# Attention into a mixture of experts on one core: the bank of halved weights built three groups apart with GpSimd's subtractions, the lists filled in the prologue, the list tiles' weights loaded before their rows

## The chip, the cores and the metric

One Trainium2 chip, one of its cores. The metric is the device time of one execution in microseconds (us); the median of three runs is compared. The core has five engines with a queue of instructions each: PE (matmuls), DVE (VectorE), ACT (ScalarE), POOL (GpSimd) and SP, which here issues DMAs only. Each works through its queue in order, and an instruction that waits holds up all that stand behind it on its engine.

## The reference

Attention over pooled keys, then a mixture of 8 experts in which each token goes to one expert.

```python
# 4 batches of 12288 tokens, width 128; kv pooled 4x4 to 768 keys per batch
kv_flat = kv_pool.reshape(B, -1, C) @ w_sr;  k = v = kv_flat
s = scale * (q @ k.transpose(0, 2, 1))
a = np.exp(s - s.max(-1, keepdims=True));  a /= a.sum(-1, keepdims=True) + 1e-09
x = (a @ v).reshape(49152, 128)
logits = x @ w_gate;  e_idx = np.argmax(logits, axis=1)          # 8 experts
probs = softmax(logits);  eom = sigmoid(x @ w_output_gate)
for e in range(E):                                               # F = 1024
    h = np.maximum(x[mask] @ w1[e], 0.0);  ye = h @ w2[e]
    out[mask] = gate_w[mask, None] * eom[mask, e, None] * ye
```

## The kernel before

The tokens are taken in 96 **groups** of 512; four groups make a **chunk** of 2048, six chunks a batch. The outer loop goes over groups `i`, each in 8 slots `s`. In group `i` the kernel computes the scores and exponentials of group `i` (`qk`, four tiles of 128 tokens), the values of group `i-1` (`pv`), the router's logits of group `i-2`, and the experts' two matmuls of group `i-8` (`moe_h`, `moe_y`), so that attention and experts of different groups share the engines. Every fp32 operand is carried as two fp16 **halves**, the rounded value and the rest; a product is three matmuls. In a tile of scores, ACT takes the exponential (`pr`, L384) and the rounded half (`ph`, L390), POOL the rest (L391), and SP transposes both through a DMA (`PT`, L401). In the experts, ACT makes `HH` (L710) and DVE `HL` (L711) from each block of PE's results; the PSUM pool `psH`, with three buffers, holds these blocks and those of `pv`, and PE can't start a block before DVE has read the one that held its buffer.

Each chunk is computed densely with the one expert that most of its tokens chose; the tokens that chose another are written as rows into **lists** in DRAM (`scr`) by 16 indirect DMAs of POOL per chunk (`scr<-rw,idx`, L588, at most one a slot, only in slots in which the counter `spare` is zero), and after the last chunk the lists are worked off in **list tiles** of 128 rows. `fill` first writes a neutral row everywhere in the lists; before the change it is a generator that begins in group 8 and issues one of its eight DMAs every third slot, and routing does not issue the first row's DMA before all eight are out (`FILLED`).

The routing of chunk `c` (small DVE operations) runs in groups `4c+5` and `4c+6` and yields the expert `ei`. `w_load` then fetches that expert's weights. For the first `NDW` chunks it fetches the raw fp32 weights and `w_split` halves them in group `4c+7`: DVE takes the largest magnitudes (L629 on `wr`), PE turns them, DVE makes a power of two (L153 to L159), ACT scales (L662) and rounds (L670), POOL subtracts (L672). Later chunks fetch ready halves from the **bank** in DRAM: `w_bank` makes the halves of all eight experts once, while the first chunks run. Its steps for one expert: two DMAs, four reductions on DVE (L629 on `wb`), the power of two, then four times ACT's rounding with the scale (L693) and DVE's subtraction with the scale (L694), and two DMAs out.

The groups of four that the windows below speak of thus have a fixed pattern: group `4c+5` (first routing group), `4c+6` (second routing group, with the reductions of `w_split` near its end), `4c+7` (split group, in which the raw weights are scaled, rounded and subtracted) and `4c+8` (free group, none of this). Keys and values of the next batch are prepared by `kv_load` and `kv_prep` (POOL sums of `kvs`, L222 to L227) over some 12 to 15 groups.

PE's, POOL's and SP's instructions stand in the order in which the code issues them; ACT's and DVE's order is the framework's scheduler's. What the generators (`w_bank`, `w_split`, `kv_prep`, `routing`) issue in a slot follows this order, and the constants in `Cfg` set their delays in slots:

```python
bk = [x for x in bk if next(x, 1) != 1]          # banks first
...
elif ws: ... next(ws, 1)                          # then the split of a chunk
... if not spare["n"] and next(kp, 1) == 1: ...   # keys, if no POOL work yet in this slot
... if x[2] in SCT and (spare["n"] if att ...): continue   # list rows, the same
```

Of the kernel before, what the change touches and what calls it, by code (L numbers as in the profile page):

```python
# [20 lines left out]
F32 = mybir.dt.float32  # L21
# [32 lines left out]
class Cfg:  # L54
# [14 lines left out]
    RSEQ = (1, 2, 1, 1)  # L69
    FS = 3  # L70
    HJ = (0, 1)
    H0 = (7, 0)
    LC = 4
    WD = 4
    NDW = 6
    BK0, BKD, BKW = 11, 2, 8
    WT = 1
# [7 lines left out]
    PHD = (0, 2)  # L85
    TB = (6, 4)


def body(ctx, tc, q, kv, w_sr, w_gate, w_og, w1, w2, out, cfg=Cfg):
# [383 lines left out]
    def routing(c):  # L473
# [108 lines left out]
        yield  # L582
        while not FILLED:
            yield
        SCT.add(c)
# [36 lines left out]
    def w_power(t, nm, hook, x=""):  # L622

        m = kvp.tile([P, 8], F32, tag="wm" + x, name=f"wm{nm}")
        m4 = kvp.tile([P, 2, 2], F32, tag="wm4" + x, name=f"wm4{nm}")
        mb = kvp.tile([P, 2, P], F32, tag="wmb" + x, bufs=1, name=f"wmb{nm}")
        for y in range(2):
            for n in range(2):
                dve.tensor_reduce(out=m4[:, y, n:n + 1], in_=t[:, n, ts(y, 512)], op=ALU.max, axis=AX.X,  # L629
                                  apply_absolute_value=True)  # L630
            yield
        dve.tensor_tensor(m[:, 0:2], m4[:, 0, :], m4[:, 1, :], op=ALU.max)
        dve.tensor_copy(mb, m[:, 0:2].unsqueeze(2).to_broadcast([P, 2, P]))
        for _ in range(cfg.WT):
            yield
        ps = []

        def turn(S):
            for n in range(2):
                pe.transpose(S[:, n, 384:512], mb[:, n, :], ident)  # L640
            ps.append(S)

        if hook:
            hooks.append(turn)
        else:
            turn(psA.tile([P, 2, 512], F32, tag="A", name=f"wps{nm}"))
        while not ps:
            yield
        largest(m[:, 0:2], ps[0][:, :, 384:512])
        powers(m[:, 2:4], m[:, 4:6], m[:, 0:2])  # L650
        dve.tensor_tensor(m[:, 6:7], m[:, 2:3], m[:, 3:4], op=ALU.mult)
        return m
# [24 lines left out]
    def w_bank(e):  # L677
# [11 lines left out]
        for n in range(2):  # L689
            w = kvp.tile([P, 2, FF], F16, tag="wbo", bufs=2, name=f"wbo{e}{n}")  # L690
            for x in range(2):
                s = slice(x * 512, x * 512 + 512)
                act.activation(w[:, 0, s], t[:, n, s], AF.Copy, scale=m[:, 4 + n:5 + n])  # L693
                dve.scalar_tensor_tensor(w[:, 1, s], t[:, n, s], m[:, 4 + n:5 + n], w[:, 0, s],  # L694
                                         op0=ALU.mult, op1=ALU.subtract)
                yield
            sp.dma_start(out=wbank[e, :, 2 * n:2 * n + 2, :], in_=w)
            yield
# [62 lines left out]
    def fill():  # L761

        f = wk.tile([P, FR, RW], F32, tag="o", name="fill")
        pool.memset(f, 0.0)
        pool.memset(f[:, :, 1:2], BIG)
        pool.memset(f[:, :, 3:4], float(GB))
        yield
        for e in range(E):
            sp.dma_start(out=scr[e * REG:(e + 1) * REG, :].rearrange("(p a b) r -> p a (b r)", p=P, b=FR),
                         in_=f.rearrange("p b r -> p (b r)").unsqueeze(1).to_broadcast([P, REG // P // FR, FR * RW]))  # L770
            yield
        FILLED.append(True)

    FILLED = []

# [45 lines left out]

    def tail_load(eri):
        e = sp.value_load(eri[0:1, 0:1], min_val=0, max_val=E - 1)
        r = sp.value_load(eri[0:1, 1:2], min_val=0, max_val=E * REG - P)
        t = kvp.tile([P, 2, FF], F32, tag="stg", name="tw")
        rw = rt.tile([P, RW], F32, tag="trw", bufs=2, name="trw")
        sp.dma_start(out=rw, in_=scr[bass.ds(r, P), :])
        sp.dma_start(out=t[:, 0, :], in_=w1[bass.ds(e, 1), :, :].rearrange("o d f -> d (o f)"))
        sp.dma_start(out=t[:, 1, :].rearrange("p (k d) -> p k d", d=C),
                     in_=w2[bass.ds(e, 1), :, :].rearrange("o (k p) d -> p (o k) d", p=P))  # L830
        return t, rw

# [49 lines left out]
    def tail_loop():  # L882
        n = nc.values_load(TL["nti"][0:1, 0:1], min_val=NST, max_val=NT // P + E)  # L883
        mark.clear()
        with tc.For_i(NST, n, 1):
            drain(tail_tile(*tail_load(tail_index(None)), along=False))

# [5 lines left out]
    with tc.manual_schedule(engines={pool.engine, sp.engine, pe.engine}):  # L893
# [6 lines left out]
        for i in (1, 2):  # L900
            q_load(i)
        q_power(0, 0, 1)
        q_prep(0)
# [4 lines left out]
        rts, kl, kp, ws, rq = [], None, None, None, None  # L908
        tix, tgen = [], []
        filler, begun = None, False  # L910
        bk, nbk = [], 0
# [20 lines left out]
        def tail_begin(x):  # L932
            g = tail_tile(*tail_load(x))
            tgen.append(g)
# [3 lines left out]
        for i in range(NG + MOE_LAG + 1):  # L938
# [6 lines left out]
            else:  # L945
                rc = None
            if i == MOE_LAG:
                filler = fill()
            for s in range(8):
                if filler and (8 * i + s) % cfg.FS == 0 and next(filler, 1) == 1:  # L950
                    filler = None
                if s == 0 and 0 <= ri < NG:
# [75 lines left out]
                if NCK - 1 in SCT and not tix:  # L1028
                    tail_prep()
                    tix = [tail_index(t) for t in range(NST)]  # L1030
                if tix and not rts and not tgen and not begun:
                    begun = True
# [46 lines left out]
```

## Time and profile before

| | |
|---|---|
| median of 3 runs | 2064.83 us (2064.72 to 2068.38) |
| profiled execution, its own time | 2063.95 us |
| its span, first to last instruction | 2062.2 us |
| mean granted TensorE clock | 0.989 of full |

The profile was taken from one execution. Between its span and its time lie 1.75 us of start and end. Windows of a trace give the busy time of every engine in a stretch of the span; the stretches below are cut where the exponential (L384) of the first tile of a group starts.

### The profile page before, as it was taken

The page shows a single profiled execution, that of the slowest core. Times are in us where ns is not written, and L with a number is a line of the kernel's source. Part 1 is how long each engine was busy: PE and PEld are TensorE (multiplying, and loading weights), DVE is VectorE, ACT ScalarE, POOL GpSimd, SP SyncE. Part 2 cuts the span into 40 slices and gives each one's busy share as a digit, 9 for nine tenths or more (in the row PEclk, how much of TensorE's full clock was granted, in tenths as well). Part 3 has the DMA queues.
Part 4 walks back from the last instruction along what each step waited for, and adds up shares of the span by engine and source line. Part 5 has one row for each costly group of instructions (what it writes and reads, how often), then busy time and mean ns, then how long its engine had stood idle before and what let it go on. Part 6 is the DMA issues. An engine that isn't in the chain of part 4 may idle for free. (4 is left out here: it accounts for less than half of the span.)

```text
span 2062.2 us, 30671 instructions
## 1 busy us (share of the span) xinstructions
PE 1916.5 (93%) x9789; PEld 976.6 (47%) x9789; DVE 1608.1 (78%) x3296; ACT 1381.6 (67%) x2470; POOL 1156.2 (56%) x995
## 2 busy tenths in 40 slices
PE   4878989798999999999999999999999999999997
PEld 2544444343444544444544544445445445445444
DVE  6788798988878778788687687787787787786673
ACT  3766767676767676776777766776776776776653
POOL 1543667666566765654656756645645645646531
PEclk9989999999999999999999999999999999999999
DMA  6979989888897887888889997977977977877712
GB/s 182 179 153 248 218 205 220 196 176 190 185 206 178 186 189 154 163 157 165 163 185 200 186 193 135 179 166 141 184 158 144 179 160 152 172 153 147 144 54 66
DMA packets 898898, 351.07 MB, mean 170 GB/s; under 512 B 822240, under 2 KB 840801, under 8 KB 898736
## 3 DMA queue, kind: packets, MB, share of 16 engines
q1 hardware_dynamic: 885824, 348.63, 81.1%
q0 software_dynamic: 12480, 0.40, 0.5%
q8 instruction: 78, 1.28, 0.3%
q14 instruction: 84, 0.69, 0.1%
q10 hardware_dynamic: 432, 0.07, 0.0%
HBM read 86.19 MB, written 62.91 MB: 72 GB/s over the span
## 5 line engine op out<-in xcount | busy, mean ns | idle before, releaser
L391 POOL TENSOR_TENSOR ph<-pr,ph 128x768 f16<-128x768 f32 x384 | 632.3, 1647 | 709.6 <-ACT ph L390 424.0
L711 DVE SCALAR_TENSOR_TENSOR HL<-H,HH 128x512 f16<-128x512 f32 x768 | 526.3, 686 | 115.8 <-ACT HH L710 103.2
L710 ACT ACTIVATE HH<-H 128x512 f16<-128x512 f32 x768 | 452.4, 590 | 213.9 <-PE H L707 211.0
L384 ACT ACTIVATE pr<-S,nm,qm 128x768 f32<-128x768 f32 x384 | 380.3, 990 | 202.3 <-DVE nm L381 163.5
L588 POOL DMA_INDIRECT scr<-rw,idx x384 | 384.3, 1001 | 93.8 <-issue 80.8
L418 PE MATMUL U<-PT,V 128*128 128x512 f16 (+1 forms) x1854 | 393.4, 367 | 33.1 <-DVE HL L711 27.9
L380 DVE TENSOR_REDUCE nm<-S 128x1 f32<-128x768 f32 x384 | 364.7, 950 | 49.8 <-PE S L377 49.2
L705 PE MATMUL H<-U,w 128*128 128x512 f16 x768 | 293.0, 381 | 31.5 <-DVE U L423 15.1
L390 ACT ACTIVATE ph<-pr 128x768 f16<-128x768 f32 x368 | 309.3, 840 | 3.6 <-issue 2.1
L721 PE MATMUL Y<-HH,w 128*128 128x512 f16 x768 | 292.3, 381 | 4.7 <-ACT ys L726 4.0
L418 PEld LDWEIGHTS <-V 128*128 128x128 f16 x1854 | 181.5, 98 | 238.8 <-issue 45.6
L723 PE MATMUL Y<-HL,w 128*128 128x512 f16 x768 | 292.2, 381 | 2.3 <-DVE HL L711 2.3
L706 PE MATMUL H<-U,w 128*128 128x512 f16 x768 | 292.8, 381 | 0.0
L707 PE MATMUL H<-U,w 128*128 128x512 f16 x768 | 292.8, 381 | 0.0
L722 PE MATMUL Y<-HH,w 128*128 128x512 f16 x768 | 292.1, 380 | 0.0
L373 PE MATMUL S<-K,qT 128*128 128x384 f16 x768 | 189.5, 329 | 9.9 <-ACT pr L384 4.7
L375 PE MATMUL S<-K,qT 128*128 128x384 f16 x768 | 189.5, 329 | 0.0
L377 PE MATMUL S<-K,qT 128*128 128x384 f16 x768 | 189.4, 329 | 0.0
L423 DVE SCALAR_TENSOR_TENSOR U<-U,U 128x512 f16<-128x512 f32 x96 | 64.8, 675 | 127.1 <-ACT U L422 127.1
L422 ACT ACTIVATE U<-U 128x512 f16<-128x512 f32 x96 | 56.8, 592 | 120.4 <-PE U L418 120.3
L706 PEld LDWEIGHTS <-w 128*128 128x128 f16 x768 | 75.3, 98 | 104.2 <-issue 42.3
L722 PEld LDWEIGHTS <-w 128*128 128x128 f16 x768 | 75.3, 98 | 96.5 <-issue 10.3
(222 smaller groups left out, 2185.2 us busy)
## 6 DMA issues: line engine op xcount, KB each, us to landing
kvs<-in_kv_dram SPq DMA_DIRECT2D x96, 256.0 KB
q<-in_q_dram SPq DMA_DIRECT2D x96, 256.0 KB
urows<-uT SPq DMA_DIRECT2D x96, 256.0 KB
out_dram<-o SPq DMA_DIRECT2D x96, 256.0 KB
w<-wbank SPq DMA_DIRECT2D x36, 512.0 KB
wb<-in_moe_w_dram SPq DMA_DIRECT2D x16, 512.0 KB
wbank<-wbo SPq DMA_DIRECT2D x16, 512.0 KB
PT<-ph SPq DMA_TRANSPOSE x384
```

The costliest lines, as they stand in the source:

```text
L380: dve.tensor_reduce(out=nm[:, 0:1], in_=S[:, :, 0:384], op=ALU.max, axis=AX.XY, negate=True)
L384: act.activation(pr.rearrange("p (a k) -> p a k", a=2), S[:, :, 0:384], AF.Exp, bias=nm[:, 1:2], scale=es, accum_out=SUMS[c][:, bl:bl + 1])
L390: act.activation(ph[:, 0, :], pr, AF.Copy)
L391: pool.tensor_tensor(ph[:, 1, :], pr, ph[:, 0, :], op=ALU.subtract)
L418: pe.matmul(PVP[i][:, cols], ops[n][0], ops[n][1][:, cols], start=(n == 0), stop=(n == len(ops) - 1))
L588: ins = pool.indirect_dma_start(out=scr, out_offset=bass.IndirectOffsetOnAxis(ap=idx[:, bl:bl + 1], axis=0), in_=rw[:, bl, :], in_offset=None,
L705: pe.matmul(H, w1h[:, ts(f, P)], UH, start=True, stop=False)
L706: pe.matmul(H, w1h[:, ts(f, P)], UL, start=False, stop=False)
L707: pe.matmul(H, w1l[:, ts(f, P)], UH, start=False, stop=True)
L710: act.activation(HH, H, AF.Relu)
L711: mark["dve"] = dve.scalar_tensor_tensor(HL, H, 0.0, HH, op0=ALU.max, op1=ALU.subtract)
L722: pe.matmul(Y, w2l[:, ts(f, P)], HH, start=False, stop=False)
```

## The change

`NDW` rises from 6 to 8, so two more chunks (6 and 7) halve their own raw weights instead of fetching ready halves. A bank begins every third group (`BKD` 3) instead of every second, the last in group 32 instead of 25, with longer delays (`BKW`, `BKT`). Its halving has another form: ACT scales in place (2 instructions of 1024 columns), ACT rounds (4 of 512), and **POOL** subtracts (4 of 512) in slots in which `spare` is zero; DVE does none of it any more. The turn of a bank's maxima goes to the end of the hooks' list. `fill` is a plain function, called in the prologue, and routing does not wait for it. The list tiles' weights are fetched 8 and 9 slots after their index is known, and only their rows when the tile begins; the pieces of a tile follow each other 3 slots apart instead of 4.

```diff
-    FS = 3
-    NDW = 6
-    BK0, BKD, BKW = 11, 2, 8
+    NDW = 8
+    BK0, BKD = 11, 3
+    BKW, BKT = 14, 3
-    TB = (6, 4)
+    TB = (6, 3)
...
         yield
-        while not FILLED:
-            yield
         SCT.add(c)
...
-        for y in range(2):
-            for n in range(2):
+        for n in range(2):
+            for y in range(2):
                 dve.tensor_reduce(out=m4[:, y, n:n + 1], in_=t[:, n, ts(y, 512)], op=ALU.max, axis=AX.X,
                                   apply_absolute_value=True)
-            yield
+                if y or x:
+                    yield
...
-        for _ in range(cfg.WT):
+        for _ in range(cfg.BKT if x else cfg.WT):
             yield
...
-            hooks.append(turn)
+            hooks.insert(0 if x else len(hooks), turn)
...
+            act.activation(t[:, n, :], t[:, n, :], AF.Copy, scale=m[:, 4 + n:5 + n])
+            yield
             for x in range(2):
                 s = slice(x * 512, x * 512 + 512)
-                act.activation(w[:, 0, s], t[:, n, s], AF.Copy, scale=m[:, 4 + n:5 + n])
-                dve.scalar_tensor_tensor(w[:, 1, s], t[:, n, s], m[:, 4 + n:5 + n], w[:, 0, s],
-                                         op0=ALU.mult, op1=ALU.subtract)
+                act.activation(w[:, 0, s], t[:, n, s], AF.Copy)
+                yield
+                while spare["n"]:
+                    yield
+                spare["n"] += 1
+                pool.tensor_tensor(w[:, 1, s], t[:, n, s], w[:, 0, s], op=ALU.subtract)
                 yield
...
-    def tail_load(eri):
+    def tail_weights(eri):
...
+    def tail_rows(eri):
+        r = sp.value_load(eri[0:1, 1:2], min_val=0, max_val=E * REG - P)
+        rw = rt.tile([P, RW], F32, tag="trw", bufs=2, name="trw")
+        sp.dma_start(out=rw, in_=scr[bass.ds(r, P), :])
+        return rw
...
         for i in (1, 2):
             q_load(i)
+        fill()
         q_power(0, 0, 1)
...
-            if i == MOE_LAG:
-                filler = fill()
             for s in range(8):
-                if filler and (8 * i + s) % cfg.FS == 0 and next(filler, 1) == 1:
-                    filler = None
...
                     tix = [tail_index(t) for t in range(NST)]
+                    for n, x in enumerate(tix):
+                        at(8 + n, lambda y: TW.append(tail_weights(y)), x)
```

Line numbers from L584 on differ between the two kernels: L711 is L715 after the change, L629 L627, L662 and L670 are L661 and L669, L672 is L671; the bank's new instructions are L690 (scale), L694 (round) and L699 (POOL's subtraction).

DVE in group 19, a split group, from the power of two of the chunk's weights on (`wm`), before the change; `wbo` are the bank's halves, `wm4b` a bank's maxima, `wmb` and `wmbb` what is made of them, `HL` the experts' rest, `nm` the scores' maxima:

```order
L159 TENSOR_SCALAR wm_4193<-wm_4193 128x2
L651 TENSOR_TENSOR wm_4193<-wm_4193 128x1
L381 TENSOR_SCALAR nm_2_4387<-nm_2_4387,qm_2102 128x1
L658 TENSOR_SCALAR msw_4351<-msc_4084,wm_4193 128x16
L711 SCALAR_TENSOR_TENSOR HL_4_4401<-H_4_4396,HH_4_4400 128x512
L694 SCALAR_TENSOR_TENSOR wbo_4409<-wb_3692,wmb_3990,wbo_4409 128x512
L711 SCALAR_TENSOR_TENSOR HL_5_4419<-H_5_4414,HH_5_4418 128x512
L694 SCALAR_TENSOR_TENSOR wbo_4409<-wb_3692,wmb_3990,wbo_4409 128x512
L741 TENSOR_TENSOR o_4378<-S_2_4377,msw_3264 128x256
L629 TENSOR_REDUCE wm4b_4550<-wb_4274 128x1 x3
L632 TENSOR_TENSOR wmb_4549<-wm4b_4550 128x2
L633 COPY wmbb_4551<-wmb_4549 128x256
```

The same place of DVE's queue now:

```order
L159 TENSOR_SCALAR wm_4182<-wm_4182 128x2
L650 TENSOR_TENSOR wm_4182<-wm_4182 128x1
L715 SCALAR_TENSOR_TENSOR HL_4_4370<-H_4_4365,HH_4_4369 128x512
L657 TENSOR_SCALAR msw_4322<-msc_4067,wm_4182 128x16
L745 TENSOR_TENSOR o_4347<-S_2_4346,msw_3270 128x256
L715 SCALAR_TENSOR_TENSOR HL_5_4385<-H_5_4380,HH_5_4384 128x512
L423 SCALAR_TENSOR_TENSOR U_4410<-U_4391,U_4410 128x512
L380 TENSOR_REDUCE nm_3_4427<-S_3_4418 128x1
L381 TENSOR_SCALAR nm_3_4427<-nm_3_4427,qm_2154 128x1
```

The two subtractions and the three reductions that stood between `HL` and the next tile's `nm` are gone from this group; a bank's reductions now stand in or between groups 11, 14 to 15, 17, 20, 23, 26 to 27, 29 and 32, its power of two in groups 14, 17, 20 and so on to 35.

ACT in group 23, also a split group, in its second half, before the change (`wr` the chunk's raw weights, `w` their halves):

```order
L384 ACTIVATE pr_2_5484,SUM_4504<-S_2_5471,nm_2_5481,qm_3181 128x768
L670 ACTIVATE w_5468<-wr_5149 128x512
L390 ACTIVATE ph_2_5486<-pr_2_5484 128x768
L670 ACTIVATE w_5468<-wr_5149 128x512
L422 ACTIVATE U_5538<-U_5519 128x512
L662 ACTIVATE wr_5149<-wr_5149,wm_5297 128x1024
L670 ACTIVATE w_5545<-wr_5149 128x512
L710 ACTIVATE HH_6_5570<-H_6_5566 128x512
L384 ACTIVATE pr_3_5560,SUM_4504<-S_3_5548,nm_3_5557,qm_3181 128x768
L670 ACTIVATE w_5545<-wr_5149 128x512
```

And now, where `wb` are a bank's raw weights:

```order
L661 ACTIVATE wr_5083<-wr_5083,wm_5241 128x1024
L690 ACTIVATE wb_4505<-wb_4505,wmb_4952 128x1024
L669 ACTIVATE w_5482<-wr_5083 128x512
L384 ACTIVATE pr_3_5497,SUM_4469<-S_3_5485,nm_3_5494,qm_3197 128x768
L714 ACTIVATE HH_6_5507<-H_6_5503 128x512
L390 ACTIVATE ph_3_5499<-pr_3_5497 128x768
L669 ACTIVATE w_5482<-wr_5083 128x512
L714 ACTIVATE HH_7_5522<-H_7_5518 128x512
L714 ACTIVATE HH_0_5559<-H_0_5555 128x512
L694 ACTIVATE wbo_5530<-wb_4505 128x512 x2
```

A bank's scaling and rounding now stand among those of the chunk's own weights, in groups 23 and 35 alike; in the other split groups they do not meet.

SP in the prologue, before (`V` and `PT` are the first transposes through DMA):

```order
L293 DMA q_179<-in_q_dram 128x512
L293 DMA q_181<-in_q_dram 128x512
L293 DMA q_311<-in_q_dram 128x512
L293 DMA q_313<-in_q_dram 128x512
L401 DMA_TRANSPOSE PT_289<-ph_0_303 128x12x128
```

And now:

```order
L293 DMA q_181<-in_q_dram 128x512
L772 DMA scr<-fill 256x1x400 x8
L293 DMA q_323<-in_q_dram 128x512
L293 DMA q_325<-in_q_dram 128x512
L401 DMA_TRANSPOSE PT_301<-ph_0_315 128x12x128
```

All eight DMAs of `fill` stand ahead of the third query load and of the first transpose. From group 42 to group 94 every engine's instructions are the same, in the same order, in both kernels.

## Rows read from the trace of the kernel before

**Rows 1.** The page: busy time of each engine, its share of the span and its instructions; and the granted clock in 40 slices of the span, in tenths.

```profile
PE 1916.5 (93%) x9789; PEld 976.6 (47%) x9789; DVE 1608.1 (78%) x3296; ACT 1381.6 (67%) x2470; POOL 1156.2 (56%) x995
PEclk9989999999999999999999999999999999999999
```

**Rows 2.** Windows of four groups each, groups 8 to 11, 12 to 15 and so on to 40 to 43: start and end, length, busy time (and instructions) of PE, PEld, DVE, ACT and POOL, then the granted clock, the DMA engines' busy share and GB/s.

```profile
139.40:228.80 89.40, 81.37 (x387) 39.22 (x386) 67.30 (x137) 58.01 (x102) 38.06 (x33) 0.93 0.98 218
228.80:323.30 94.50, 82.68 (x414) 41.34 (x412) 80.73 (x165) 64.89 (x116) 64.03 (x55) 0.98 0.95 215
323.30:417.80 94.50, 81.41 (x411) 40.63 (x409) 84.70 (x165) 64.75 (x118) 64.49 (x57) 1.00 0.89 201
417.80:512.30 94.50, 82.31 (x404) 40.73 (x402) 78.69 (x178) 65.89 (x117) 62.82 (x55) 0.96 0.86 183
512.30:601.00 88.70, 81.91 (x404) 40.49 (x403) 75.43 (x158) 63.27 (x112) 46.65 (x40) 0.98 0.90 191
601.00:682.20 81.20, 77.06 (x395) 39.02 (x393) 63.92 (x123) 55.63 (x103) 58.54 (x52) 1.00 0.86 188
682.20:763.20 81.00, 78.64 (x403) 39.92 (x402) 63.77 (x123) 55.70 (x102) 53.10 (x47) 1.00 0.88 182
763.20:846.00 82.80, 78.73 (x401) 39.60 (x400) 66.81 (x134) 56.63 (x104) 52.71 (x46) 1.00 0.79 161
846.00:924.40 78.40, 77.29 (x395) 38.99 (x394) 61.62 (x123) 55.23 (x99) 42.92 (x36) 1.00 0.87 165
```

**Rows 3.** Windows of single groups, the same columns: group 16 (free), 18 (second routing group, with a chunk's reductions), 19 (split group), 26 (second routing group, with reductions), 27 (split group), 30 (second routing group, without), 31 (the group at a split group's place, without a split), 38 (second routing group in which `kv_prep` ends).

```profile
323.30:342.70 19.40, 18.22 (x95) 9.38 (x93) 11.94 (x21) 13.48 (x25) 16.22 (x15) 1.00 0.85 177
367.00:392.50 25.50, 21.25 (x103) 9.96 (x101) 25.09 (x51) 15.36 (x28) 14.32 (x12) 1.00 0.93 197
392.50:417.80 25.30, 20.33 (x101) 10.07 (x102) 23.81 (x45) 19.59 (x35) 17.54 (x18) 1.00 0.83 198
554.80:578.50 23.70, 19.48 (x92) 9.09 (x91) 22.59 (x52) 15.17 (x29) 6.05 (x4) 0.98 0.75 166
578.50:601.00 22.50, 21.32 (x101) 10.51 (x100) 19.25 (x39) 19.25 (x33) 15.28 (x16) 0.94 1.03 224
642.10:662.80 20.70, 18.03 (x90) 8.74 (x89) 19.86 (x44) 15.23 (x27) 12.31 (x10) 1.00 0.86 191
662.80:682.20 19.40, 19.40 (x101) 9.91 (x100) 12.59 (x23) 13.58 (x26) 15.30 (x17) 1.00 0.87 176
804.30:829.20 24.90, 21.46 (x108) 10.46 (x107) 24.18 (x58) 17.73 (x34) 10.53 (x11) 1.00 0.76 171
```

**Rows 4.** Waits in groups 10 and 11 (178 to 229 us): who waited for whom, us in total, times, the longest; and the two groups' windows.

```profile
ACT q L331 <- DMA qT<-q: 4.6, 1, 4.6
DVE wm4b L629 <- DMA wb<-in_moe_w_dram: 4.1, 1, 4.1
DVE wm L629 <- DMA wr<-in_moe_w_dram: 1.6, 1, 1.6
178.40:205.00 26.60, 21.34 (x95) 9.73 (x94) 20.10 (x49) 15.19 (x28) 7.21 (x7) 0.88 1.07 259
205.00:228.80 23.80, 21.02 (x98) 9.97 (x96) 17.43 (x35) 17.28 (x29) 13.48 (x14) 0.91 0.97 219
```

**Rows 5.** Group 14: one DVE instruction and one of PE in the timeline (start, us, instruction, and the idle time before it with what ended it), and the window behind them.

```profile
291.97 0.18 DVE L572 SCALAR_TENSOR_TENSOR idx<-sel,ix 128x16 int32<-128x16 f32 x1 [3.01 <-DMA scr<-rw,idx]
295.24 0.59 PE L705 MATMUL H<-U,w 128*128 128x512 f16 x1 [4.57 <-DVE U L423]
295.20:303.00 7.80, 7.07 (x28) 3.12 (x28) 7.06 (x19) 5.47 (x10) 3.60 (x7) 0.83 0.16 31
```

**Rows 6.** `fill`'s DMAs (issue times min, median, max in ns, first and last start in us), two windows of the prologue, and SP's first transpose in the timeline.

```profile
L769 SPq DMA_DIRECT2D scr<-fill x8: 587/882/1692, 149.6 to 213.9; - x8
16.00:24.00 8.00, 4.34 (x11) 2.47 (x11) 6.17 (x15) 2.27 (x9) 0.00 (x0) 1.00 1.03 380
24.00:42.00 18.00, 9.00 (x29) 4.22 (x30) 12.58 (x35) 5.08 (x11) 1.64 (x1) 1.00 0.01 4
40.74 1.55 SPq L401 DMA_TRANSPOSE PT<-ph  x1
```

**Rows 7.** The weights' instructions by line: durations min, median, max in ns, first and last start in us. The last row, for L694, is one of the groups by line: count, busy us, mean ns, idle time before.

```profile
L629 DVE TENSOR_REDUCE wm4b<-wb x32: 669/675/687, 214.6 to 549.5; 128x1 f32<-128x512 f32 x32
L672 POOL TENSOR_TENSOR w<-wr,w x20: 1145/1154/1281, 219.7 to 601.4; 128x512 f16<-128x512 f32 x20
L693 ACT ACTIVATE wbo<-wb,wmb x32: 707/720/757, 253.2 to 588.3; 128x512 f16<-128x512 f32 x32
L662 ACT ACTIVATE wr<-wr,wm x12: 1132/1140/1151, 133.7 to 594.3; 128x1024 f32<-128x1024 f32 x12
L670 ACT ACTIVATE w<-wr x20: 616/618/630, 219.0 to 596.4; 128x512 f16<-128x512 f32 x20
L694 DVE SCALAR_TENSOR_TENSOR wbo<-wb,wmb,wbo 128x512 f16<-128x512 f32 x32 | 28.8, 901 | 0.3 <-ACT wbo L693 0.2
```

**Rows 8.** Two small DVE instructions by line, the columns of rows 7.

```profile
L159 DVE TENSOR_SCALAR wmb<-wmb x8: 169/200/1500, 253.0 to 583.1; 128x2 int32<-128x2 int32 x8
L538 DVE TENSOR_TENSOR z<-z,rinv x24: 143/156/1608, 108.1 to 1973.0; 128x16 f32<-128x16 f32 x24
```

**Rows 9.** The end: PE's last transpose chain and the last DMA of a list tile in the timeline.

```profile
2045.13 0.33 PE L852 MATMUL tps<-ident,tu 128*128 128x128 f32 x1
2048.79 2.01 PE L866 MATMUL tY<-tw,tHs 128*128 128x128 f32 x16
2051.47 1.00 POOL L874 DMA_INDIRECT out_dram<-tov,ttk  x1 [1.51 <-DVE tov L872]
```

More of the change, by code (lines that the diff above doesn't have):

```diff
@@ L766, in fill @@
         pool.memset(f[:, :, 3:4], float(GB))
-        yield
         for e in range(E):
@@ L770, in fill @@
                          in_=f.rearrange("p b r -> p (b r)").unsqueeze(1).to_broadcast([P, REG // P // FR, FR * RW]))
-            yield
-        FILLED.append(True)
-    FILLED = []
     def tail_prep():
@@ L820, in tail_index @@
         return eri
-    def tail_load(eri):
+    def tail_weights(eri):
         e = sp.value_load(eri[0:1, 0:1], min_val=0, max_val=E - 1)
-        r = sp.value_load(eri[0:1, 1:2], min_val=0, max_val=E * REG - P)
         t = kvp.tile([P, 2, FF], F32, tag="stg", name="tw")
-        rw = rt.tile([P, RW], F32, tag="trw", bufs=2, name="trw")
-        sp.dma_start(out=rw, in_=scr[bass.ds(r, P), :])
         sp.dma_start(out=t[:, 0, :], in_=w1[bass.ds(e, 1), :, :].rearrange("o d f -> d (o f)"))
@@ L830, in tail_load @@
                      in_=w2[bass.ds(e, 1), :, :].rearrange("o (k p) d -> p (o k) d", p=P))
-        return t, rw
+        return t
+    def tail_rows(eri):
[3 more added lines that the diff above has]
+        return rw
     def tail_tile(t, rw, along=True):
@@ L885, in tail_loop @@
         with tc.For_i(NST, n, 1):
-            drain(tail_tile(*tail_load(tail_index(None)), along=False))
+            x = tail_index(None)
+            drain(tail_tile(tail_weights(x), tail_rows(x), along=False))
     def drain(g):
@@ L908, in body @@
         rts, kl, kp, ws, rq = [], None, None, None, None
-        tix, tgen = [], []
-        filler, begun = None, False
+        tix, tgen, TW = [], [], []
+        begun = False
         bk, nbk = [], 0
@@ L932, in tail_begin @@
         def tail_begin(x):
-            g = tail_tile(*tail_load(x))
+            g = tail_tile(TW.pop(0), tail_rows(x))
             tgen.append(g)
```

## The prediction

> **What bounds the kernel now.** I read the page first: PE is busy for 93% of the span, no other engine above 78%, and the clock is granted almost throughout [rows 1]. So time can be won only where PE waits. The windows of four groups say where: groups 40 to 43 take 78.4 us, groups 12 to 23 take 94.5 three times, groups 24 to 27 88.7, and 28 to 39 about 81 to 83 [rows 2]. The same attention and expert work stands in all of them. What the slow ones have besides is DVE work: 80.7, 84.7, 78.7 and 75.4 us against 61.6. Single groups show how that bites: group 18 is 25.5 us long with DVE busy for 25.1 of them, while the free group 16 takes 19.4 with DVE at 11.9 [rows 3]. In the weights' era DVE's queue sets the length of three groups in four, and PE waits since its blocks in `psH` are read late. The change touches groups 8 to 41, the prologue and the tail alone; the order of all else is the same.
>
> Two stalls have another origin. In groups 10 and 11 ACT waited 4.6 us for a transposed query, DVE 4.1 and 1.6 us for raw weights, with the DMA engines at 1.07 and 0.97 busy, and PE's clock at 0.88 and 0.91 [rows 4]. `fill`'s DMAs run just then, from 149.6 to 213.9 us [rows 6]. In group 14 DVE waited 3.01 us until the list rows of an older chunk, held back by `FILLED`, had left the buffer `idx`; PE then stood for 4.57 us, and got 0.83 of the clock, so partly its 1.2 GHz level, over the next 7.8 us [rows 5].
>
> **The change part by part.**
>
> *Fill.* Groups 10 and 11 take 50.4 us [rows 4]; the same pair of kinds, 26 and 27, takes 46.2 with as much weights' work [rows 3]. I take these 4.2 us, and 3.0 for group 14, whose wait goes when the first list rows leave in groups 7 to 9: **-7.2**. Bounds: 0 if other DMAs arrive just as late; -14.9 if all waits named go in full (10.3 and 4.57). In the prologue the price is 0: between 24 and 42 us DMA is idle (0.01), and eight DMAs of 410 KB, 3.3 MB, take 8.6 us at the 380 GB/s of the stretch before, so they land before the first transpose at 40.7 [rows 6]. At the 182 GB/s of groups 32 to 35 [rows 2] they would take 18 us, and the first transposes would be late by 1.3 us; with no cover at all they would be late by the whole 8.6.
>
> *Two more splits* (chunks 6 and 7). A split's reductions lengthen the second routing group: 23.7 against 20.7, or 25.5 against 20.7, so 3.0 to 4.8; in the split group the difference is 22.5 against 19.4, 3.1, but that group has a bank's subtractions too [rows 3]. I take 3.9 and 1.1, 5 us a split: **+10**, between 6 (3.0 each) and 16 (4.8 and 3.1 each).
>
> *The banks.* Above equals without weights' work (81.1 where keys are prepared, 78.4 where not), groups 12 to 27 lose 3 x 13.4 + 10.3 = 50.5 us [rows 2]. Four splits at 5 leave 30.5, or 3.8 us for each of eight banks. On DVE a bank costs four subtractions of 0.90, four reductions of 0.675 [rows 7] and about 2 us of small instructions (an estimate: some ten of 0.2, now and then one of 1.5 [rows 8]), 8.3 in all. The subtractions leave DVE, 43% of it: -13.1. Of the 17.4 left, about half now stands where DVE has room (the order puts four of eight sets of reductions, and four of eight powers of two, into free groups or into split groups whose subtractions are gone; DVE has 7.5 us to spare in group 16 [rows 3]): -8.7. Against this, ACT's part grows from 4 x 0.72 = 2.9 to 2 x 1.14 + 4 x 0.618 = 4.8 us [rows 7]. That hides where ACT has 13.5 of 19.4 us [rows 3], not in groups 23 and 35, where bank and split meet: 13.6 + 9.5 = 23.1 us of ACT in order, against about 20.5 with a split alone, +5 for the two.
>
> POOL gets 32 x 1.154 = 36.9 us more [rows 7]; it has room, but DVE pays: L538 takes 0.156 us as a rule and 1.608 at worst, L159 0.200 and 1.500 [rows 8], the length of a POOL instruction. The price comes from the keys' sums: groups 28 to 35 have 25.8 us more POOL work than twice groups 40 to 43, and are 5.4 us longer [rows 2], 0.21 us for each us of POOL: +7.7. Together the banks give -13.1 - 8.7 + 5 + 7.7 = **-9.1**, between 0 and -20. The Trainium skill speaks against this move (SBUF — State Buffer, Who interferes with whom): GpSimd and a DVE instruction with two SBUF inputs, or in a two-port mode, exclude each other for a whole instruction, while a reduction never contends. The long cases of L538 and L159 agree with the lock; read at its worst, with a DVE instruction behind each of the 32, the banks would come to +20 instead of -9.1.
>
> *Keys.* With POOL's slots taken, the end of the second `kv_prep` moves from group 38, which takes 24.9 us against 20.7 for group 30 [rows 3], to the free group 40. Group 39 already gives some of it back: four groups take 82.8 against 81.1 [rows 2], so **-1.7** (0 to -4.2).
>
> *Tail.* The last 5.7 us of PE are the second list tile alone, from 2045.13 on [rows 9]. Its first half now stands ahead of the last output's transposes: **-1**, between -2 and +1.5, if the gather of its rows, issued with less time to land, holds up DVE. Loading weights early gives nothing, since no wait for them is seen.
>
> Sum: -7.2 + 10 - 9.1 - 1.7 - 1 = -9.0, on the profiled execution's 2063.95 us: 2055. The median lies 0.9 above that execution; I expect the new one at 2056.
>
> **The rivals.**
>
> *The banks go nearly free* (0.17): DVE was the only bound, and what remains of a bank hides. For it: groups as long as DVE's busy time [rows 3]. Against it: half of the remaining pieces still stand in routing groups. -20 instead of -9.1, so 2045, at best 2038.
>
> *ACT takes DVE's place* (0.17): ACT's queue has 25 us more in groups 11 to 36 (banks 8 x 1.9, splits 2 x 4.75), in order, with `HH` behind each wait for a power of two. If a bank costs 3.8 us as before, the total is 2055.8 + 9.1 = 2065, no change.
>
> *POOL blocks DVE* (0.14), the other side: 0.24 us per moved subtraction is in the sum. Without it the sum is -16.7, so it decides for slower from 0.65 us each on (20.8 us), of at most 1.154; at 0.75 the time is 2065 + 7 = 2072. For it: the worst cases [rows 8]. Against it: the keys' sums cost DVE a fifth of that. The rule named above, at its worst, is this rival in full: 36.9 us, 2085.
>
> *The change as summed* (0.52): 2047 to 2061.
>
> **How the numbers follow.** The predicted time is that of the last case. Its own range is 2047 to 2061, by the bounds of fill and splits. For 8 in 10 the range takes in half of the free-bank case and the no-change case: 2045 to 2068. A measurement of this kernel tells about 0.2%, 4 us, from no change. Faster than 2060.7 are the forecast and the free banks, 0.69; same 0.17; slower 0.14.
>
> **What the profile should show.** Groups 8 to 11: near 85 us, no wait for `qT` or for `idx`, clock near 1. Groups 12 to 27 together about 20 us shorter than their 372; group 19 near 20.5. Groups 28 to 35 about 14 longer than their 162, groups 30 and 34 near 24. Groups 23 and 35 near 23 to 24, with ACT busy for 22. DVE's small instructions beside L699 tell POOL's price: more of them at 1.2 us, and the third rival is right. Groups 42 to 94 unchanged. The prediction is wrong if ACT's wait for the power of two moves into PE's blocks, if bank reductions in groups 14 and 26 cost as much as before, or if `fill` delays the first transposes.

## The result and the profile after

The change made the kernel slower: 2077.51 us (median of 4; 2075.1 to 2080.55) against 2065.68 us for the kernel before on the same chip (median of 4), a ratio of 1.0056 with a 95% interval of 1.0041 to 1.0072, or +11.6 us, slower by more than the 0.2% that a measurement tells. The prediction was 2056 (2045 to 2068). The profiled execution took 2075.1 us, with a span of 2073.4.

The page of the changed kernel, busy time of each engine and the granted clock; it answers [rows 1]:

```profile
PE 1924.1 (93%) x9793; PEld 979.6 (47%) x9793; DVE 1608.4 (78%) x3284; ACT 1404.2 (68%) x2498; POOL 1196.7 (58%) x1035
PEclk9989999999999999999999999999999999999999
```

DVE is as busy as before (1608.4 against 1608.1), although 28.8 us of bank subtractions left it: the two more splits (5.5 us of reductions), and small instructions that take longer, took their place: `msw` (L657) takes 8.3 us for 8, before 1.4 for 6. The windows of four groups, 8 to 11 up to 40 to 43, with the columns of [rows 2]:

```profile
140.20:227.10 86.90, 78.92 (x387) 38.34 (x386) 67.75 (x137) 58.38 (x103) 54.30 (x47) 0.98 0.91 187
227.10:317.60 90.50, 84.00 (x416) 42.08 (x415) 73.09 (x145) 64.30 (x114) 59.20 (x52) 0.96 0.93 201
317.60:406.80 89.20, 80.87 (x400) 40.15 (x399) 72.81 (x145) 63.93 (x114) 63.37 (x57) 0.96 0.88 189
406.80:505.50 98.70, 82.79 (x409) 40.90 (x408) 83.98 (x170) 68.56 (x123) 61.35 (x54) 0.98 0.78 170
505.50:590.30 84.80, 79.59 (x403) 39.70 (x402) 68.85 (x145) 63.35 (x112) 53.62 (x46) 1.00 0.88 190
590.30:678.70 88.40, 79.77 (x397) 39.83 (x395) 71.98 (x145) 63.81 (x113) 61.91 (x55) 0.96 0.87 194
678.70:771.60 92.90, 82.87 (x405) 41.09 (x404) 75.95 (x151) 67.87 (x121) 59.88 (x53) 0.96 0.82 176
771.60:851.60 80.00, 78.24 (x405) 40.22 (x404) 61.22 (x123) 56.47 (x106) 61.84 (x55) 1.00 0.92 191
851.60:931.40 79.80, 78.14 (x397) 39.11 (x396) 67.28 (x135) 56.05 (x101) 45.88 (x39) 1.00 0.83 164
```

Against [rows 2], groups 8 to 11 won 2.5 us (4.2 were forecast), 12 to 27 won 9.0 (20), 28 to 35 lost 19.1 (14), 36 to 43 won 1.4 (1.7). The rest is +0.8 ahead of group 8, +2.2 in groups 44 to 94, whose work is the same, and +2.0 behind them. Groups 28 to 31 and 32 to 35 are the odd ones: 88.4 and 92.9 us long with DVE busy for only 72.0 and 76.0, where [rows 2] has it busy for 79 to 85 in 94.5. So DVE's work alone is not what made them long. DVE's waits for a bank's raw weights (in total, times, the longest), before and then after, four rows of group 29 in the timeline (start, duration, instruction, in brackets the idle time before it and what ended it), and that group's window show one thing that did:

```profile
DVE wm4b L629 <- DMA wb<-in_moe_w_dram: 9.0, 6, 4.1
DVE wm4b L627 <- DMA wb<-in_moe_w_dram: 16.8, 8, 5.4
612.92 0.34 SPq L679 DMA_DIRECT2D wb<-in_moe_w_dram  x1
616.24 0.28 DVE L488 TENSOR_TENSOR d<-L,mx 128x128 f32<-128x128 f32 x1
618.92 0.69 DVE L627 TENSOR_REDUCE wm4b<-wb 128x1 f32<-128x512 f32 x1 [2.40 <-DMA wb<-in_moe_w_dram]
623.28 1.01 PE L418 MATMUL U<-PT,V 128*128 128x512 f16 x2 [4.44 <-DVE HL L715]
609.40:636.80 27.40, 22.96 (x110) 11.21 (x109) 24.07 (x49) 17.87 (x33) 14.72 (x12) 0.88 0.83 202
```

The code asks for a bank's reductions `BKW` = 14 slots, some 35 us, behind the load. But DVE's order is not that of the code: the scheduler put the reduction 6.0 us behind the load's issue. The weights were not there, DVE stood for 2.40 us in order with the routing behind it, `HL` came late, PE stood for 4.44 us, and the clock was 0.88 in the group. Before, such waits are 9.0 us in all (the longest is in [rows 4]).

Group 32 shows a second thing. It is 4.8 us longer than before, and PE's longest wait there is over before DVE's wait for `wb`, which ends at 687.71 us, could touch it:

```profile
680.90 2.12 DVE L154 TENSOR_SCALAR wmb<-wmb 128x2 f32<-128x2 f32 x1
683.45 1.15 ACT L690 ACTIVATE wb<-wb,wmb 128x1024 f32<-128x1024 f32 x1 [1.23 <-DVE wmb L159]
684.99 0.98 ACT L384 ACTIVATE pr<-S,nm,qm 128x768 f32<-128x768 f32 x1
686.11 0.56 PE L742 MATMUL S<-ident,ys 128*128 128x128 f32 x2 [2.71 <-ACT pr L384]
```

DVE's power of two came late, ACT stood before the bank's new scaling (L690) with the exponential `pr` behind it, and PE stood for `pr`. In group 20 the same wait of ACT stands ahead of 2.1 us of PE's for `ys` (L730).

### The profile page after: what moved, and what is told of

Same layout as the page of the kernel before. It is cut to its first block, busy times and chain, and to the rows that moved or that the text cites. A ratio compares the mean times of both kernels' runs of the same rounds, so it can differ in the third digit from the quotient of the medians.

```text
span 2073.4 us, 30727 instructions
## 1 busy us (share of the span) xinstructions
PE 1924.1 (93%) x9793; PEld 979.6 (47%) x9793; DVE 1608.4 (78%) x3284; ACT 1404.2 (68%) x2498; POOL 1196.7 (58%) x1035
## 4 chain that ended last, share of the span: by engine, by line
PE 50%; DVE 27%; issue 8%; DMA 6%; ACT 5%; POOL 2%; SPq 1%; ACTq 0%; DVEq 0%; POOLq 0%
PE U L418 11%; DVE HL L715 5%; DVE nm L380 5%; PE H L709 4%; PE H L711 4%; PE H L710 4%; PE Y L725 4%; PE Y L726 4%; PE Y L727 4%; PE S L373 3%; PE S L377 3%; PE S L375 3%; ACT pr L384 1%; DVE x L560 1%; DMA wb<-in_moe_w_dram 1%
## 5 line engine op out<-in xcount | busy, mean ns | idle before, releaser
L715 DVE SCALAR_TENSOR_TENSOR HL<-H,HH 128x512 f16<-128x512 f32 x768 | 525.8, 686 | 128.4 <-ACT HH L714 115.9
L418 PE MATMUL U<-PT,V 128*128 128x512 f16 (+1 forms) x1854 | 399.1, 370 | 38.6 <-DVE HL L715 34.3
L709 PE MATMUL H<-U,w 128*128 128x512 f16 x768 | 292.5, 381 | 19.7 <-DVE HL L715 15.5
L711 PE MATMUL H<-U,w 128*128 128x512 f16 x768 | 292.5, 381 | 0.0
L711 PEld LDWEIGHTS <-w 128*128 128x128 f16 x768 | 75.3, 98 | 92.2 <-issue 1.4
```

Of the source, the lines that this page charges most:

```text
L418: pe.matmul(PVP[i][:, cols], ops[n][0], ops[n][1][:, cols], start=(n == 0), stop=(n == len(ops) - 1))
L709: pe.matmul(H, w1h[:, ts(f, P)], UH, start=True, stop=False)
L711: pe.matmul(H, w1l[:, ts(f, P)], UH, start=False, stop=True)
L715: mark["dve"] = dve.scalar_tensor_tensor(HL, H, 0.0, HH, op0=ALU.max, op1=ALU.subtract)
```

## The experiments

Theory A: what costs is DVE standing in order before weights that have not landed. Theory B: GpSimd blocks DVE (the third rival). Theory C: the two further splits. Times are ratios to the kernel before on the same chip, in brackets their 95% interval. The chip of e1 to e4 took 2082 us for the kernel before (in the traces of all four, and of no other run, PE stands for 11 to 13 us near 2.0 ms), the others 2065. 0.001 is 2.07 us.

**The parts of the change, each alone.** e2_fill: the `fill` hunks of the diff. e3_splits: one line. e4_bank: that and the hunks on banks.

```diff
-    NDW = 6
+    NDW = 8
```

> The kernel before, with fill's eight DMAs moved into the prologue and FILLED taken out, and nothing else. By the prediction's sum -7.2 us: 2058.5 against 2065.7, with groups 8 to 11 near 85 us. By the trace of the changed kernel, where groups 8 to 11 lost 2.5 and group 14 1.9 us, and the prologue and the first groups gained 1.5: -3, about 2062.5. If the waits of groups 10 and 11 only move to other transfers, no change.

Measured: 0.9993 (0.9983 to 1.0003), -1.5 us. Group 10 lost 2.5 us and group 14 4.1, as forecast; but list rows now leave GpSimd in groups 9 and 11, which grew by 1.2 and 1.1, group 15 took back 1.5, and in this trace the stretch ahead of group 8 is 2.4 us longer. The window of groups 0 and 1, and the one in which `fill` now lands, in this kernel, and then group 1 of e5_tail, in which `fill` is late as before:

```profile
37.30:61.30 24.00, 19.02 (x97) 10.71 (x96) 16.35 (x36) 15.12 (x27) 12.02 (x8) 0.86 0.74 138
24.00:42.00 18.00, 9.68 (x29) 4.45 (x30) 12.31 (x34) 5.00 (x11) 1.64 (x1) 1.00 0.57 184
```

```profile
47.60:60.80 13.20, 12.19 (x71) 7.61 (x69) 7.59 (x18) 7.47 (x15) 7.15 (x5) 0.79 1.05 179
```

The transfers do fit the idle stretch (0.57 of 18 us is 10.3, where 8.6 were estimated), yet the clock was 0.86 behind it. `fill` isn't shown to be the cause: in e8_fillord, with the same `fill`, the clock was 1.00 there and the stretch ahead of group 8 only 0.7 us longer, and in e5_tail, without it, group 1 got 0.79 and took 13.2 us, against 11.7 before. Between e13_ord and e8_fillord, below, the same move is worth -3.9 us.

> The kernel before, with NDW = 8 in place of 6 and nothing else: chunks 6 and 7 split their weights instead of loading them from the bank. By the prediction's sum +10 us: 2076, in groups 30, 31, 34 and 35 (5 us for each pair). If the splits are the cause of the loss (theory C), more than that, up to 2080; by theory A, 6 to 10, since the second routing groups 30 and 34 of the changed kernel grew by 2.2 and 2.6 us only, and the split groups 31 and 35 of it hold a bank's work too.

Measured: 1.0030 (1.0018 to 1.0042), +6.2 us, at the low bound of the forecast. The splits by themselves can't carry the loss.

> The kernel before, with NDW = 8 and the new form of the banks (scaling and halving on ACT, 32 subtractions on GpSimd, BKD 3, BKW 14, BKT 3), and with fill and the list tiles as they were. Less the run with NDW = 8 alone this is what the banks' new form and places are worth. By the prediction's sum -9.1 us against that run, so 2067. By theory A (reductions that wait for their weights, more often than before: 16.8 against 9.0 us) between 0 and +4 against it, so 2076 to 2080. By theory B (GpSimd blocks DVE, 0.65 us and more each): +5 to +15 against it.

Measured: 1.0066 (1.0052 to 1.0080). Less e3_splits the banks' new form costs +7.5 us (about 4 to 11 by the two intervals) where -9.1 was forecast, or -10.8 with the keys' -1.7, which this run holds too: here is the error. The number itself lies in theory B's range and above theory A's; DVE's waits for `wb` are 16.0 us in its trace, as theory A had them. The runs that follow take the two apart.

**The list tiles alone.** e5_tail: the hunks on `tail_weights`, `tail_rows` and `TB`.

> The kernel before with the change of the list tiles alone (weights loaded 8 and 9 slots after tail_index, TB = (6, 3)). By the prediction -1 us (between -2 and +1.5). By the profiled executions so far, whose stretch behind group 94 is 2.0 us longer with the new list tiles than with the old ones on the first chip and 4 to 5 us longer on the second, +2 to +5.

Measured: 1.0001 (0.9992 to 1.0010): nothing beyond the interval, of 2 us to either side. Its trace is 1.9 us longer behind group 94, as that of the changed kernel is.

**The wait taken away.** e1_ordred and e9_ordred2 are one kernel, the changed one with

```diff
-                dve.tensor_reduce(out=m4[:, y, n:n + 1], in_=t[:, n, ts(y, 512)], ...
+                with behind() if x else ExitStack(): dve.tensor_reduce(
```

> The changed kernel, in which each of the four reductions of a bank is kept behind the last HL or nm instruction of the slot in which the code asks for it. Nothing else is changed; DVE's queue then has one such reduction per slot, 14 slots and more behind the weights' DMAs, where before it had them up to ten slots earlier. Theory A (DVE stands in order behind reductions whose raw weights have not landed, and PE's blocks in psH are read late): DVE's 16.8 us of waits for wb go to under 2, groups 11, 17, 20, 29 and 32 lose 1 to 4 us each, and the time falls by 8 to 15 us against the changed kernel, to 2063 to 2070. Theory B (GpSimd's 32 subtractions block DVE): the waits go, the time stays within 3 us of the changed kernel's 2077.5, since the subtractions stay where they are. Theory C (the two further splits and ACT's longer part cost it): the same as B.

> The kernel of e1_ordred once more, since e1_ordred ran on a chip on which the kernel before took 2082 us, and e6_ordsub and e7_nosub on one on which it took 2065. By the profiled executions, whose groups 8 to 41 are 742.8 us long in e1_ordred, 739.4 in e6_ordsub and 745.8 before, and whose end behind group 94 is about 2 us longer than before: the same as the kernel before, 1.000 (0.998 to 1.001), 3 to 4 us slower than e6_ordsub. If e1_ordred's 1.0019 holds on any chip, 1.002.

Measured: 1.0019 (1.0010 to 1.0028) and 1.0005 (0.9996 to 1.0015). No wait for `wb` of a reduction is left, and against the changed kernel's 1.0056 it wins 0.0051, 10.5 us (7.7 by e1_ordred). So most of what lifts the change above the kernel before is this wait. It doesn't explain why nothing is won: without it 1.0005 is left, where 2056 would be 0.995. In e9_ordred2 groups 11, 17 and 29 fall from the changed kernel's 25.0, 26.3 and 27.4 us to 20.8, 20.5 and 21.6. Groups 20 and 32 do not: 24.5 and 24.0 become 23.4 and 25.0 (before the change 19.1 each), and PE's waits for ACT in them stay, with 2.0 and 3.0.

**The wait put back.** e10_late: `BKW` 1 and banks begun 13 slots later, so the reductions stand where e9_ordred2 has them.

```diff
-                if s == 0 and i >= cfg.BK0 and (i - cfg.BK0) % cfg.BKD == 0 and nbk < E:
+                if s == 5 and i > cfg.BK0 and (i - cfg.BK0) % cfg.BKD == 1 and nbk < E:
```

> The kernel of e1_ordred with each bank's weights loaded 13 slots later (BKW 1 in place of 14, begun 13 slots later), so that the reductions stand at the same places of DVE's queue, two to six slots behind the issue. Theory A (what costs is DVE standing in order before weights that have not landed): waits for wb of 1 to 4 us per bank come back, 10 to 25 us in all, and the time rises against e9_ordred2 by 4 to 12 us. If it was the spreading of the reductions over slots that won, and not the wait, the same time as e9_ordred2.

Measured: 1.0099 (1.0084 to 1.0115), 19.4 us more than e9_ordred2. DVE's wait in its trace:

```profile
DVE wm4b L627 <- DMA wb<-in_moe_w_dram: 20.0, 8, 4.9
```

20.0 us of waits and 19.4 us of time, more than the 12 expected at most, with DVE's order nearly kept (27 of its 3284 instructions stand elsewhere): theory A holds, and it isn't the spreading of the reductions that won.

**The price of the subtractions.** e6_ordsub and e7_nosub are e9_ordred2 with `dve.` for `pool.` in the subtraction, and without it. e11_bnosub is the kernel before without it.

```diff
-                pool.tensor_tensor(w[:, 1, s], t[:, n, s], w[:, 0, s], op=ALU.subtract)
+                dve.tensor_tensor(w[:, 1, s], t[:, n, s], w[:, 0, s], op=ALU.subtract)
```

> The kernel of the run e1_ordred, with the banks' 32 subtractions on DVE in place of GpSimd, at the same slots. By the prediction's terms (13.1 us for the subtractions on DVE, 7.7 for GpSimd's price) it is 5.4 us slower than e1_ordred, 1.0045 of the kernel before. If GpSimd's subtractions block DVE (the third rival), it is faster than e1_ordred by 5 us and more, 0.999 or less. If DVE has room for them once no reduction waits, the same, 1.002.

> The kernel of the run e1_ordred without the banks' 32 subtractions: the low halves are left out, and the high halves are written to the bank twice. What it wins against e1_ordred is the whole price of the subtractions on GpSimd. By the prediction 7.7 us, so 0.998 of the kernel before; if GpSimd's work is free to the others, 1.002 as e1_ordred; if it blocks DVE as the third rival has it (0.65 us and more for each), 20 us, 0.992.

Measured: 0.9992 (0.9983 to 1.0001) and 0.9958 (0.9944 to 0.9971). Against e9_ordred2, on GpSimd they cost 9.7 us, 0.30 each (forecast: 0.24, and 0.65 for the third rival), so theory B's price isn't there; on DVE 7.0 there. Which engine is better in this kernel the intervals don't tell.

> The kernel before without the banks' 32 subtractions on DVE: the low halves are left out, and the high halves are written to the bank twice. What it wins is what the subtractions cost on DVE at the places that they have before. By the prediction 13.1 us, 0.9937; if they cost there what they cost in e6_ordsub against e7_nosub by the groups 8 to 41, 4 us, 0.998.

Measured: 0.9988 (0.9979 to 0.9997), -2.5 us for 28.8 us of DVE work left out. DVE's wait for the banks' weights in its trace:

```profile
DVE wm4b L629 <- DMA wb<-in_moe_w_dram: 22.6, 10, 4.1
```

From 9.0 to 22.6: with the subtractions gone, DVE came to the next reduction sooner and stood there. Two runs without that wait settle it: e13_ord is the kernel before with the edit of e1_ordred, e14_ordnosub that without the subtractions.

> The kernel before with the banks' reductions kept behind the marks of their slots, and nothing else (fill late, as before). If the 9.0 us of waits for wb in before cost as those of e10_late did (19 us of time for 20 us of waits) or as those of the changed kernel did (10.5 for 16.8): 0.9955 to 0.9975 of the kernel before. e8_fillord, which has fill early too, is at 0.9964.

> The kernel of e13_ord without the banks' 32 subtractions: the low halves are left out, and the high halves are written to the bank twice. Its gain against e13_ord is the price of the subtractions on DVE where no reduction waits. If e11_bnosub's gain of 2.5 us was small since the work left out was replaced by waits, it is now 8 to 13 us (0.4 to 0.6%), near the prediction's 13.1. If DVE has room for the subtractions, it is 2 to 4 us again.

Measured: 0.9983 (0.9974 to 0.9992) and 0.9930 (0.9917 to 0.9944). The waits of before cost 3.5 us, less than expected; and where no reduction waits, the subtractions are worth 10.9 us on DVE, near the 13.1 of the prediction.

**Better kernels.** e8_fillord is e13_ord with `fill` early; e12_bk10 and e16_bk12 have `BK0` 10 and 12 in it; e15_poolsub gives it the change's hunks on banks, and:

```diff
-    BK0, BKD, BKW = 11, 2, 8
+    BK0, BKD = 11, 2
+    BKW, BKT = 5, 1
```

> The kernel before with fill moved as in e2_fill and the banks' reductions kept behind the marks of their slot as in e1_ordred, everything else of before (NDW 6, subtractions on DVE, old list tiles). Theory A (reductions that wait for their weights hold DVE's queue): 9.0 us of waits for wb in before go, and a part of them shows in the time, -3 to -8 us besides fill's -1.5, so 0.995 to 0.998. If the waits in before cost nothing, 0.999 as e2_fill.

Measured: 0.9964 (0.9950 to 0.9977), as expected. It is also the kernel to hold e9_ordred2 against: both have `fill` early and no wait for `wb`, and e9_ordred2 is 0.0041, 8.5 us, slower. The splits are 6.2 of that, so without any wait the banks' new form and places gained nothing there.

> The kernel of e8_fillord with each bank begun one group earlier (BK0 10 in place of 11), so that the reductions stand in split groups and first routing groups in place of free groups and second routing groups, where group 18 of e8_fillord had DVE busy for all of its 29.3 us. If DVE's room in the group decides what a bank costs, 3 to 8 us faster than e8_fillord, 0.993 to 0.995 of the kernel before; if not, 0.996 as e8_fillord.

> The kernel of e8_fillord with each bank begun one group later (BK0 12 in place of 11): reductions in first routing and split groups as in e12_bk10, but their subtractions one and two groups later. If the reductions' groups decide, as e12_bk10: 0.9998. If it was the subtractions' groups that made e12_bk10 slow, or the load of raw weights in groups 10 and 11 that fell together with it, 0.996 as e8_fillord or better.

Measured: 0.9998 (0.9989 to 1.0007) and 1.0004 (0.9995 to 1.0013), both slower than e8_fillord. For e12_bk10 this is against the expectation; e16_bk12 came out like e12_bk10, as expected for the case that the reductions' groups decide. But more than the reductions moved: both kernels have a bank's power of two, roundings and four subtractions in free groups and second routing groups, where e8_fillord has only its four reductions. PE's waits for the column that the reductions fill, in e8_fillord and then in e16_bk12:

```profile
PE S L638 <- DVE wmb L631: 1.2, 1, 1.2
```

```profile
PE S L638 <- DVE wmb L631: 11.9, 4, 3.8
```

PE's transposes of a bank stand a fixed count of slots behind the reductions in PE's order, and with the new places DVE fills the column late. But these waits don't carry the loss: each ends 1.5 us into a split group (15, 19, 23, 27), and these groups with those ahead of them are together only 0.6 us longer than in e8_fillord. The free groups 16, 20, 24 and 28 grew, by 2 to 4 us each. Group 16 in e8_fillord and then in e16_bk12:

```profile
318.10:337.50 19.40, 17.43 (x89) 8.91 (x89) 15.17 (x27) 13.83 (x26) 16.56 (x15) 1.00 0.84 177
314.00:336.30 22.30, 19.49 (x97) 9.57 (x96) 19.75 (x31) 15.91 (x29) 16.49 (x15) 1.00 1.00 205
```

In each of the four DVE has 4 to 9 us more work, and ACT stands 1.2 to 2.2 us for a bank's power of two. So the pieces that moved in made the free groups longer, and did not hide in DVE's room; whether by DVE's work or by ACT's wait no run here tells.

> The kernel of e8_fillord with the banks in the new form (scaling and halving on ACT, subtractions on GpSimd; BKW 5, BKT 1 so that all banks are done in time; BKD 2 and NDW 6 as before). By the prediction's terms the subtractions leave DVE for -13.1 and cost +7.7 on GpSimd and some on ACT: 3 to 5 us faster than e8_fillord, 0.994. By e6_ordsub against e9_ordred2 (DVE 0.9992, GpSimd 1.0005): 2 to 4 us slower than e8_fillord, 0.998.

Measured: 0.9935 (0.9921 to 0.9948), 2052.60 us: faster than both kernels, by 13 and 25 us. Its page, and its subtractions on GpSimd:

```profile
PE 1913.3 (93%) x9789; PEld 976.3 (48%) x9789; DVE 1594.5 (78%) x3264; ACT 1393.9 (68%) x2486; POOL 1188.2 (58%) x1027
L700 POOL TENSOR_TENSOR wbo<-wb,wbo 128x512 f16<-128x512 f32 x32 | 37.5, 1171 | 0.3
```

The new form wins 6.0 us here against e8_fillord (some 2 to 10 by the intervals): a sign like the prediction's, and against the expectation taken from e6_ordsub. This kernel and the changed one without its waits differ in `BKD`, `BKW`, `BKT`, the list tiles and the splits; which of these turns the comparison is open.

## Why the prediction was wrong

**What bounds the kernel.** That time is lost between groups 8 and 41, for the most part in DVE's order, was right. That DVE's *busy time* sets the lengths was not enough: [rows 3] has group 18 with 25.09 of 25.5 us busy, but in group 32 of the changed kernel DVE is busy for 17.3 of 23.9.

**The failing step is the sum for the banks**, -9.1 forecast, +7.5 measured. It shares out 30.5 us of loss by DVE's busy time ("The subtractions leave DVE, 43% of it: -13.1") and has no term for a wait at a reduction. The row was there: [rows 4] has DVE waiting 4.1 us for `wb`. It was put down to `fill`'s traffic; with `fill` gone from those groups the wait in group 11 is still 5.4 us. The 30.5 us themselves hold 4.8 us of such waits, and the 3.0 us of group 14 that the term for `fill` had taken already.

Term by term, the runs showed this in its place:

- The *wait* has no term. It costs 10.5 us in the changed kernel and 3.5 in the kernel before, so about +7.
- The *subtractions leaving DVE*, -13.1, are worth 10.9 where no reduction waits, and 7.0 at the change's places. Where a reduction waits they are worth 2.5, since DVE then comes to it sooner and stands there.
- *GpSimd's price*, +7.7, measured 9.7.
- The *pieces that hide* (-8.7) and *ACT's longer part* (+5), with the keys -5.4 in all, no run has apart. But e7_nosub and e14_ordnosub, both without subtractions and without waits, differ by +5.8 us; of this the splits are 6.2, the list tiles 0.2 and `fill` -1.5 to -3.9. That leaves +1 to +3, an estimate from runs on several chips, each with an interval of 2 to 3 us to either side.

So the wait is a little under half of the 16.6 us by which the banks were missed, and most of the rest is that the moved pieces did not hide. Groups 20 and 32 show one place: ACT stands for a power of two ahead of PE's blocks. The prediction's second rival and the first of its signs of being wrong name this; here it is read from traces, and no run tested it.

**GpSimd's price** was nearly right, in the order of e9_ordred2 (by groups 8 to 41, 742.8 us in e1_ordred against 735.2 in e7_nosub, it is 7.6). The third rival's side, slower, came true, but not its mechanism: 0.30 us a subtraction is far below the 0.65 from which it decides. The prediction let a subtraction hold DVE for at most its own 1.154 us; a trace has a hold of 5.58 us, see below. The Trainium skill (SBUF — State Buffer, Who interferes with whom) says that, where a DVE and a GpSimd instruction contend for the ports that the two engines share, whichever issues first has them for the whole instruction and the other is blocked; that trace has DVE held, but for longer than one instruction.

**Splits** +10, measured +6.2, the low bound. **Fill** -7.2, measured -1.5 alone and -3.9 where no reduction waits: most of the stalls named went, but part of it came back where list rows now leave, a price that the sum has no term for. **Keys** -1.7, by the windows -1.4. **List tiles** -1, measured +0.2. With the banks as measured the sum is -1.5 + 6.2 + 7.5 + 0.2 = +12.4, against +11.6 for the whole.

**Of the profile forecast**: groups 8 to 11 at 86.9 (85) without a wait for `idx`, though with 1.5 us of the one for `qT`, group 19 at 19.7 (20.5), groups 30 and 34 at 22.9 and 22.7 (24), groups 23 and 35 at 23.3 and 25.3 with ACT at 20.7 and 21.4 (23 to 24, 22), were near. Groups 12 to 27 and 28 to 35, -9.0 and +19.1 where -20 and +14 were forecast, were not: groups 17, 20, 29 and 32, which no step spoke of, grew by 2.0, 5.4, 5.2 and 4.8.

## What to carry to other kernels

An engine's queue is in order, and a yield in the code is no place in it: look up where the scheduler put an instruction that needs a transfer, and how long behind the transfer's issue it stands. Work taken off an engine is worth little while the next instruction there waits for something else (2.5 us here in place of 10.9), so before a price is put on removed work, see whether a wait will move up into its place. Work moved to an engine with room does not hide if it waits there in order ahead of what PE needs. Keeping four small instructions of each bank behind a mark took the change from +0.56% to +0.05% (+0.19% on the other chip); the banks' new form with that, with `fill` early, and with the old splits, spacing and list tiles gains 0.65%.

## What the runs showed of the hardware

A small DVE instruction can be held for a whole run of GpSimd instructions, not for one alone. `sume` (L482, 128x16) by line in e7_nosub, without the banks' subtractions, and in e9_ordred2, with them (min, median, max in ns), the second with its longest case in the timeline:

```profile
L482 DVE TENSOR_SCALAR sume<-SUM,ve x24: 284/285/1342, 80.7 to 1936.7; 128x16 f32<-128x16 f32 x24
```

```profile
L482 DVE TENSOR_SCALAR sume<-SUM,ve x24: 283/285/5579, 81.1 to 1948.4; 128x16 f32<-128x16 f32 x24
576.72 1.17 POOL L699 TENSOR_TENSOR wbo<-wb,wbo 128x512 f16<-128x512 f32 x1
577.36 5.58 DVE L482 TENSOR_SCALAR sume<-SUM,ve 128x16 f32<-128x16 f32 x1
577.83 1.16 POOL L671 TENSOR_TENSOR w<-wr,w 128x512 f16<-128x512 f32 x1
578.94 1.64 POOL L391 TENSOR_TENSOR ph<-pr,ph 128x768 f16<-128x768 f32 x1
580.54 1.15 POOL L671 TENSOR_TENSOR w<-wr,w 128x512 f16<-128x512 f32 x1
581.65 1.25 POOL L222 TENSOR_TENSOR kvs<-kvs 128x512 f32<-128x512 f32 x1
582.85 0.68 DVE L715 SCALAR_TENSOR_TENSOR HL<-H,HH 128x512 f16<-128x512 f32 x1
```

GpSimd's instructions follow each other without a gap until 582.90 us, and `sume` ends at 582.94: 5.58 us for an instruction of 0.285. It began during a bank's subtraction (L699), and four more GpSimd instructions followed. Group 27, where this stands, is 24.9 us long against 21.2 without the subtractions. e1_ordred has the same case with 5.63 us, and e10_late two, of 5.54 and 5.81, each begun during an L699; the changed kernel itself has none, its longest hold of a small DVE instruction is 2.42 us. The traces show the hold; which lock makes it no run here can tell.
